# Pairs 4 to 7 of an MLP: transposes on TensorE replaced by a strided reload and 32x32 block transposes on VectorE

## The chip, the core and the metric

The kernel runs on one core of one Trainium2 chip. The metric is the device time of one execution in microseconds (us); the number that counts is the median of several runs. Every figure of an engine, a wait or a transfer comes from one profiled execution.

## The reference, cut to what matters

A transformer block over 2048 tokens of 640 features: a LayerNorm, an attention with a learned feature map, and a second LayerNorm with an MLP (640 to 1728 to 640, squared ReLU). Scale and shift of both norms (`ca`, `sa`, `cb`, `sb`) and both gates come from a small modulation vector.

```python
x = x + ga * attention(layernorm(x) * (1 + ca) + sa)     # x1
h = layernorm(x) * (1 + cb) + sb                         # per token, over 640 features
r = relu(h @ w1 + b1)
x = x + gb * ((r * r) @ w2 + b2)
```

The LayerNorm needs tokens on the partitions (its sums run along the features), while the matrix product with `w1` needs features on the partitions. Between the two, each tile of tokens has to be turned round. The change is about how that is done.

## The kernel before, in words

The attention fills the first 380 us. The MLP then works on pairs of token tiles: pair `j` is 256 tokens, there are eight pairs (0 to 7). All of it is written out in one order by hand (the engines' queues are in program order), in the last loop of the kernel: for pair `j` it goes through seven steps `n`, each with two blocks of 128 hidden features, so fourteen half-steps 0 to 13. In half-step `f`, TensorE computes `up(j, f)` (line 78 by way of `mm`): 15 matmuls of 128x256, three for each of five 128-feature chunks, since each operand is split into a high and a low part. ScalarE applies bias and ReLU (`ft<-up`, L1255), VectorE squares (L1256), ScalarE and VectorE split the result into high (`ra` L1279, `rs` L1295) and low (L88), and TensorE multiplies by `w2` one step later (`acc`). From pair 2 on the second product uses seven block products per step (`down_pair`), whose weights come in from HBM through four ring buffers that GpSimd fetches (`t_fetch`, L1365).

Beside this, while pair `j` is multiplied, pair `j+1` is prepared. `layer(j+1, at)` is called once in each half-step `at`, and the tables `LN_AT0` to `LN_AT` say what is due in which one. For pairs 4 to 7 the table is `LN_AT`, and the work is:

- half-step 0: `load_xm` and `load_xx` load the attention's result (`xm`) and the raw input (`xx`), token tiles of 128x640, by the SP queue.
- half-steps 3 and 4: `add_x` adds the two tiles on VectorE (L1079); the sum is x1, which SP also stores to HBM (`X1`, L1080) for the residual that is needed an iteration later (`residual`, `xr<-x`, L1414).
- half-steps 4 to 7: `ln_pieces` on ScalarE: two sums (L1503), two sums of squares (L1508), and after three small GpSimd operations (L1510 to L1512) two scalings in place (L1515). The sums' unneeded outputs go into `xx`.
- half-steps 8, 10 and 12: `t2`: TensorE transposes two, two and one 128-feature chunks (`t_in`, L357, two transposes for each chunk, into the PSUM tile `tb`); `t_out` applies the modulation on ScalarE (L368, out of PSUM into `xx`), copies to the high part `h` (L369), and VectorE makes the low part (L88 `h<-xx`).

The next pair's `up` reads `h` from half-step 0 on. A chunk `d` is the features 128d to 128d+127, and `w1`'s rows and the modulation's columns `cols_b` are laid out by the same chunks (`mod_turn` transposes the summed modulation rows, parts 3 and 4 being those of `cols_b`).

`row("s1", ...)` hands out five rotating buffers of 128x640; before the change an iteration takes four of them (two `xx`, two `xr`).

Of the kernel before, what the change touches and what calls it, by code (L numbers as in the profile page):

```python
# [22 lines left out]
NC = D // P  # L23
# [9 lines left out]
EPS = 1e-5  # L33
# [2 lines left out]
KEPT = NT - POSTPONED  # L36
W2_AT = 48
PLAIN = 2
DIRECT = 2
LAST = 3  # L40
W_AT = (
# [10 lines left out]
def kernel(  # L52
# [19 lines left out]
    nc = tc.nc  # L72
# [14 lines left out]
    def lo(out_lo, full, hi, eng=None):  # L87
        (eng or nc.vector).tensor_tensor(out_lo, full, hi.bitcast(F32), op=ALU.subtract)  # L88
# [10 lines left out]
    tiny = ctx.enter_context(tc.tile_pool(name="tiny", bufs=1))  # L99
# [17 lines left out]
    def row(tag, name):  # L117
        return (pc if tag in ("s3", "s4") else mem).tile([P, D], F32, tag=tag, name=name, bufs=BUFS[tag])
# [13 lines left out]
    def small(shape, tag, name, bufs=2):  # L132
        return (pc if tag in ("mx", "sk", "dn", "dd") else tiny).tile(shape, F32, tag=tag, name=name, bufs=bufs)
# [4 lines left out]
    def tp(name):  # L138
        return psA.tile([P, 512], F32, tag="tp", name=name)
# [20 lines left out]
    ident = const.tile([P, P], F32, name="ident")  # L160
# [5 lines left out]
    mhalf = const.tile([P, 2], F32, name="mhalf")  # L166
# [4 lines left out]
    cols_b = const.tile([P, 10], F32, name="cols_b")  # L171
# [128 lines left out]
    def mod_turn(part, p, *cs_):  # L300
        t = MT.setdefault(part, None) or row("s1", f"mt{part}")
        MT[part] = t
        a, n = cs_[0] * P, len(cs_) * P
        for i, c in enumerate(cs_):
            nc.tensor.transpose(p[:, i * P : (i + 1) * P], MA[part][:, c * P : (c + 1) * P], ident)
        nc.scalar.activation(t[:, a : a + n], p[:, :n], AF.Copy)

    def mod_sum(part, dest):
# [8 lines left out]
    MA = {}  # L317
# [34 lines left out]
        for _ in ln_parts(xt, nm, spare):  # L352
            pass

    def t_in(xn, d, p):
        for i in range(2):
            nc.tensor.transpose(p[:, i * P : (i + 1) * P], xn[:, i, d * P : (d + 1) * P], ident)  # L357

    def t_unit(xn, cols, hT, d, nm, p=None):
        if p is None:  # L360
            p = tp(f"t{nm}_{d}")
        t_in(xn, d, p)
# [13 lines left out]
    X1 = [dram.tile([P, 2, D], F32, name=f"x1_{j}") for j in range(NT // 2)]  # L376
# [336 lines left out]
    for t in range(2, NT - 2):  # L713
        j, i = divmod(t, 2)
# [12 lines left out]
        p = proj("v", t, (1, 0, lambda: t1(j + 1, 4)) if t == NT - 3 else None)  # L727
# [76 lines left out]
    def bank(nm):  # L804
        return psB.tile([P, 512], F32, tag="m", name=nm)
# [145 lines left out]
    def num_lo(j):  # L951

        if j >= DIRECT:
            for b, (src, hi, low) in enumerate(num_parts(j)):
# [77 lines left out]
    todo = {"load": list(preps), "hi": list(preps), "lo": list(preps)}  # L1032
# [21 lines left out]
    XM, H2, R2 = {}, {}, {}  # L1054

    XX = {}
# [25 lines left out]
    def t2(j, *ds):  # L1082
        if 0 in ds:
            H2[j] = ht(f"h2_{j}", j, (0, 96))
        if j == 0:
            t_unit(XM[j], cols_b, H2[j], ds[0], f"b{j}", bank(f"tb{j}_{ds[0]}"))
            return
        p = tp(f"tb{j}_{ds[0]}")
        for k, d in enumerate(ds):
            t_in(XM[j], d, p[:, 256 * k : 256 * k + 256])  # L1090
# [42 lines left out]
    for j in range(NB):  # L1133
        nxt = j + 1 < NB
        b, c = 2 * j + 5, 2 * j + 6
# [51 lines left out]
        if j == 7:  # L1187
            t2(0, 4)
            p = tp("gbt")[:NC, :P]
# [73 lines left out]
    def plain(j, n):  # L1263
        return j < PLAIN or n == NF // 2 - 1 or j == NB - 1 and n >= NF // 2 - LAST

# [224 lines left out]
    LN2 = {}  # L1490
# [1 line left out]
    LN_AT0 = {"load": 2, "xx": 3, "add": (5, 6), "ln": (5, 6, 7, 7, 8, 9), 10: (0, 1), 11: (2, 3), 12: (4,)}  # L1492
    LN_AT1 = {"load": 3, "add": (5, 5), "ln": (5, 6, 6, 7, 8, 8), 9: (0, 1), 11: (2, 3), 12: (4,)}
    LN_AT2 = {"load": 0, "xx": 3, "add": (6, 6), "ln": (7, 7, 8, 8, 9, 9), 10: (0, 1), 11: (2, 3), 12: (4,)}
    LN_AT = {"load": 0, "add": (3, 4), "ln": (4, 5, 6, 6, 7, 7), 8: (0, 1), 10: (2, 3), 12: (4,)}
    PREPS = iter([1, 3] + [2, 1, 2, 2, 1, 2] + [1, 1] + [1, 2])

    def ln_pieces(xt, nm, spare):
        sm = small([P, 2], "sm", f"sm{nm}")
        sq = small([P, 2], "sq", f"sq{nm}")  # L1500
        nb = small([P, 2], "nb", f"nb{nm}")
        for i in range(2):
            nc.scalar.activation(spare[i], xt[:, i], AF.Identity, accum_out=sm[:, i : i + 1])  # L1503
            if i:
                nc.gpsimd.tensor_scalar(sm, sm, -1.0 / D, None, op0=ALU.mult)
            yield
        for i in range(2):
            nc.scalar.activation(spare[i], xt[:, i], AF.Square, bias=sm[:, i : i + 1], accum_out=sq[:, i : i + 1])  # L1508
            if i:
                nc.gpsimd.tensor_scalar(sq, sq, 1.0 / D, EPS, op0=ALU.mult, op1=ALU.add)  # L1510
                nc.gpsimd.tensor_tensor(sq, sq, mhalf, op=ALU.pow)
                nc.gpsimd.tensor_tensor(nb, sm, sq, op=ALU.mult)  # L1512
            yield
        for i in range(2):
            nc.scalar.activation(xt[:, i], xt[:, i], AF.Identity, bias=nb[:, i : i + 1], scale=sq[:, i : i + 1])  # L1515
            yield

    def layer(j, at, part=None):
        todo = {1: LN_AT0, PLAIN: LN_AT1, PLAIN + 1: LN_AT2}.get(j, LN_AT)
        if j == NB:  # L1520
            return
        if part != 1:
            if at in todo:
                t2(j, *todo[at])
            if todo["load"] == at:
                load_xm(j)
            if todo.get("xx", todo["load"]) == at:
                load_xx(j)
            for i in range(2):
                if todo["add"][i] == at:  # L1530
                    add_x(j, i)
        if part == 0:
            return
        for i in range(6):
            if todo["ln"][i] == at:
                if i == 0:
                    LN2[j] = ln_pieces(XM[j], f"b{j}", XX[j])
                next(LN2[j])

    for j in range(NB):  # L1540
        if j <= PLAIN:
# [4 lines left out]
        for n in range(NP):  # L1546
# [13 lines left out]
            if j < PLAIN:  # L1560
                layer(j + 1, 2 * n, None if j else 0)
# [141 lines left out]
```

## Time and profile before

| what | value |
|---|---|
| median of 3 runs | 766.31 us (765.49 to 766.42) |
| time of the profiled execution | 766.05 us |
| its span in the profile | 764.3 us (1.7 us lie around it) |
| TensorE matmul busy | 758.5 us, 99% of the span |
| VectorE / ScalarE / GpSimd busy | 78% / 57% / 19% |
| granted TensorE clock | 1.00 in each of the four stages looked at (522.8 to 706.7 us) |

Times in the timelines below are microseconds from the span's start. A timeline line gives the start, the length and the instruction, and in square brackets how long its engine had been idle and what ended that. A line of the groups gives, after the bar, the busy time of the whole group in us, the mean length of one instruction in ns, and the idle time before the group. The half-steps of pair 3, in which pair 4 is prepared, lie at 527.8 to 573.6 us; pairs 4, 5 and 6 follow at about 46 us each, and pair 7, in which nothing more is prepared, ends the program.

### The profile page before, as it was taken

What the parts mean: (1) busy time and instruction counts of PE and PEld (TensorE: products, weight loads), DVE (VectorE), ACT (ScalarE), POOL (GpSimd) and SP (SyncE); (2) the same over time, 40 slices, a digit from 0 to 9 for tenths busy, and PEclk for the clock granted to TensorE, in tenths of its full rate; (3) what the DMA queues carried; (4) which work ended last, traced back from release to release, by engine and by line L of the source; (5) the groups of instructions that cost most, each with busy time, mean ns of one, the idle gap of its engine ahead of it and who ended that gap; (6) DMA issues with size and microseconds to landing.
All of it is one profiled execution on the core that took longest, in us unless ns stands there. A gap on an engine that the chain in (4) does not pass through costs nothing.

```text
span 764.3 us, 15303 instructions
## 1 busy us (share of the span) xinstructions
PE 758.5 (99%) x5968; PEld 739.7 (97%) x5968; DVE 593.9 (78%) x1083; ACT 435.6 (57%) x972; POOL 144.9 (19%) x301
## 2 busy tenths in 40 slices
PE   9999999999999999999999999999999999999997
PEld 8999999999999989988999999999999999999997
DVE  6598897988999899999655667876767666685666
ACT  5766756677853364546776647465563645536331
POOL 3001101001100255432101000231321313213110
PEclk9999999999999999999999999999999999999999
DMA  8811431343332345223366466996766759767460
GB/s 322 329 61 78 138 104 54 104 136 112 126 104 93 109 150 188 72 87 104 122 194 221 120 227 236 283 334 209 224 166 207 232 179 268 199 184 204 126 184 35
DMA packets 51505, 126.69 MB, mean 166 GB/s; under 512 B 6684, under 2 KB 7457, under 8 KB 51433
## 3 DMA queue, kind: packets, MB, share of 16 engines
q1 hardware_dynamic: 34098, 84.65, 32.8%
q0 software_dynamic: 14752, 35.76, 16.9%
q10 hardware_dynamic: 2583, 5.30, 1.8%
q8 instruction: 47, 0.77, 0.5%
q14 instruction: 25, 0.20, 0.1%
HBM read 95.70 MB, written 29.89 MB: 164 GB/s over the span
## 4 chain that ended last, share of the span: by engine, by line
PE 91%; DVE 7%; DMA 1%; issue 0%; SPq 0%; ACT 0%; DVEq 0%
PE up L78 24%; PE acc L78 18%; PE pq L78 9%; PE pk L78 9%; PE pv L78 9%; PE pwo L78 6%; PE acc3x L78 5%; PE kvp L450 3%; PE te L920 1%; DVE dn L878 1%; DVE scr L876 1%; DVE ezb L900 1%; PE tb L357 1%; PE ta L357 1%; DVE ot L88 1%; PE foldq L280 1%
## 5 line engine op out<-in xcount | busy, mean ns | idle before, releaser
L78 PE MATMUL up<-h,w 128*128 128x256 f32 x1640 | 206.4, 278 | 0.0
L78 PEld LDWEIGHTS up<-h,w 128*128 128x128 f32 x1640 | 196.1, 188 | 0.0
L1255 ACT ACTIVATE ft<-up,b_t 128x256 f32<-128x256 f32 x104 | 49.1, 472 | 113.8 <-PE up L78 113.2
L78 PE MATMUL acc<-w,ra 128*128 128x384 f32 x452 | 97.4, 335 | 0.0
L1256 DVE TENSOR_TENSOR ft<-ft 128x256 f32<-128x256 f32 x104 | 44.1, 424 | 48.4 <-ACT ft L1255 46.8
L78 PE MATMUL pwo<-wo,ot 128*128 128x256 f32 (+3 forms) x512 | 80.5, 312 | 0.1
L78 PEld LDWEIGHTS pwo<-wo,ot 128*128 128x128 f32 (+1 forms) x512 | 74.4, 188 | 3.2 <-issue 2.7
L78 PE MATMUL pq<-wq,hT 128*128 128x384 f32 (+1 forms) x480 | 75.2, 312 | 0.0
L78 PEld LDWEIGHTS acc<-w,ra 128*128 128x128 f32 x452 | 72.7, 188 | 0.8 <-DVE ra L88 0.5
L78 PE MATMUL pk<-wk,hT 128*128 128x384 f32 (+1 forms) x480 | 72.7, 308 | 0.0
L78 PE MATMUL pv<-wv,hT 128*128 128x384 f32 (+1 forms) x480 | 71.7, 307 | 0.0
L78 PEld LDWEIGHTS pq<-wq,hT 128*128 128x128 f32 x480 | 71.1, 188 | 0.6 <-issue 0.2
L78 PEld LDWEIGHTS pk<-wk,hT 128*128 128x128 f32 x480 | 70.5, 188 | 0.4 <-issue 0.2
L78 PEld LDWEIGHTS pv<-wv,hT 128*128 128x128 f32 x480 | 70.1, 188 | 0.0
L88 DVE TENSOR_TENSOR ra<-ft,ra 128x384 fp32r<-128x384 f32 (+2 forms) x86 | 36.8, 449 | 32.6 <-ACT ra L1279 19.3
L1365 POOL DMA_DIRECT2D ring_a<-td_a x34 | 18.3, 539 | 126.1 <-PE acc L78 100.4
L1279 ACT ACTIVATE ra<-ft 128x384 fp32r<-128x384 f32 x48 | 25.2, 526 | 28.4 <-DVE ft L1256 22.4
L78 PE MATMUL acc3x<-w,ra 128*128 128x256 f32 x231 | 39.8, 278 | 0.0
L78 PEld LDWEIGHTS acc3x<-w,ra 128*128 128x128 f32 x231 | 37.2, 188 | 0.2 <-DVE ra L88 0.2
L1270 DVE TENSOR_TENSOR ft<-ft 128x128 f32<-128x128 f32 x136 | 33.4, 287 | 1.2
L441 DVE TENSOR_REDUCE sk<-ek 128x64 f32<-128x1280 f32 x16 | 23.7, 1484 | 12.4 <-ACT ek L436 10.8
L884 POOL TENSOR_TENSOR dn<-dn,rs_q 128x32 f32<-128x32 f32 x32 | 20.2, 630 | 66.7 <-DVE dn L878 66.4
(270 smaller groups left out, 1412.6 us busy)
## 6 DMA issues: line engine op xcount, KB each, us to landing
ring_c<-td_c POOLq DMA_DIRECT2D x34, 384.0 KB, 4.2
ring_a<-td_a POOLq DMA_DIRECT2D x34, 384.0 KB, 4.1
ring_b<-td_b POOLq DMA_DIRECT2D x34, 256.0 KB, 4.0
esp<-eq SPq DMA_DIRECT2D x12, 640.0 KB, 3.0
el<-esp SPq DMA_DIRECT2D x12, 640.0 KB, 3.9
rw<-in_w SPq DMA_DIRECT2D x23, 320.0 KB, 2.9
wm<-in_w_mod SPq DMA_DIRECT2D x20, 320.0 KB, 3.3
xb<-in_x SPq DMA_DIRECT2D x8, 640.0 KB, 4.2
```

The lines of the kernel that those rows point to most:

```text
L78: nc.tensor.matmul(o, a, b, start=first and i == 0, stop=last and i == len(terms) - 1, skip_group_check=skip,)
L88: (eng or nc.vector).tensor_tensor(out_lo, full, hi.bitcast(F32), op=ALU.subtract)
L280: nc.tensor.matmul(p[g // 3][:, (g % 3) * 120 : (g % 3) * 120 + n], r, bd_t[:120, g * 120 : g * 120 + n], start=True, stop=True,)
L357: nc.tensor.transpose(p[:, i * P : (i + 1) * P], xn[:, i, d * P : (d + 1) * P], ident)
L441: nc.vector.tensor_reduce(s, heads(flat(e)), axis=AX.X, op=ALU.add)
L450: nc.tensor.matmul(kvp[g // 4][64 * c : 64 * c + 64, a : a + 2 * n].rearrange("p (s n) -> p s n", s=2), v[:, u], e[:, :, o : o + n], start ...
L884: nc.gpsimd.tensor_tensor(dn[:, s], dn[:, s], rs[:, 1 - s], op=ALU.mult)
L1255: nc.scalar.activation(r, p, AF.Relu, bias=b1_t[:, f : f + 1])
L1256: nc.vector.tensor_tensor(r, r, r, op=ALU.mult)
L1270: nc.vector.tensor_tensor(t[:, o], t[:, a], t[:, b], op=op)
L1279: nc.scalar.activation(a[:, 0, :3], t[:, :3], AF.Copy)
L1365: nc.gpsimd.dma_start(RING[j, n, r], TD[n][r].bitcast(F32R))
```

## The change

For pairs 4 to 7 (`DEALT = 4`) no transpose is left on TensorE. Instead:

- `add_x`'s second tile moves from half-step 4 to 3, and the sums and squares move to half-steps 4, 4, 5 and 5. Their unneeded outputs go to a fifth row of `s1` (`junk`).
- half-step 5: `load_dealt` reads x1 back from HBM into `xx`, eight DMAs of 32 partitions: partition 32q+t gets, for each of four groups `a` of 32 tokens, the 160 features 160q to 160q+159 of token 32a+t.
- half-step 6: the two LayerNorm factors of each token are copied between partitions, 16 VectorE copies of 32x4, so that partition 32q+t holds those of the tokens 32a+t.
- half-steps 7 and 8: eight scalings of 128x160 on ScalarE, in place in `xx`.
- half-steps 8 and 9: `turn`: one VectorE transpose in 32x32 blocks for each token tile, from `xx` (read with a step of 5 elements, 20 bytes) into `xm`. The feature that ends on partition p of chunk b is 5p+b.
- half-steps 10, 11 and 12: `t_out` for two, two and one chunks, now out of SBUF, in place in `xm`.

Chunks are therefore the features 5p+b, for all pairs. `w1` is laid out so on the host. Pairs 0 to 3 still transpose on TensorE, now reading every fifth element (`by_turn`), 40 transposes; so do the ten of `mod_turn` for parts 3 and 4.

```diff
+DEALT = 4
...
+            src = by_turn(MA[part])[:, c] if part in (3, 4) else MA[part][:, c * P : (c + 1) * P]
+            nc.tensor.transpose(p[:, i * P : (i + 1) * P], src, ident)
...
+    def by_turn(ap):
+        return ap.rearrange("p (f b) -> p b f", b=NC)
...
+    def t_in(xn, d, p, mixed=False):
         for i in range(2):
-            nc.tensor.transpose(p[:, i * P : (i + 1) * P], xn[:, i, d * P : (d + 1) * P], ident)
+            src = by_turn(xn[:, i])[:, d] if mixed else xn[:, i, d * P : (d + 1) * P]
+            nc.tensor.transpose(p[:, i * P : (i + 1) * P], src, ident)
...
+        if j >= DEALT:
+            for d in ds:
+                hf = XM[j].rearrange("p s d -> p (s d)")[:, 256 * d : 256 * d + 256]
+                t_out(cols_b, H2[j], d, f"b{j}", hf, hf)
+            return
...
+    def load_dealt(j):
+        for i in range(2):
+            for q in range(4):
+                nc.sync.dma_start(
+                    XX[j][i][32 * q : 32 * q + 32].rearrange("t (a c) -> t a c", a=4),
+                    X1[j][:, i, 160 * q : 160 * q + 160].rearrange("(a t) c -> t a c", a=4),
+                )
+
+    def turn(j, i):
+        xt = XM[j].rearrange("p s d -> p (s d)").rearrange("p (b i a t) -> p i a b t", b=NC, i=2, t=32)
+        nc.vector.transpose(xt[:, i], XX[j][i].rearrange("p (a t b) -> p a b t", a=4, t=32))
...
-    LN_AT = {"load": 0, "add": (3, 4), "ln": (4, 5, 6, 6, 7, 7), 8: (0, 1), 10: (2, 3), 12: (4,)}
+    LN_AT = {"load": 0, "add": (3, 3), "dealt": 5, "ln": (4, 4, 5, 5, 6, 7, 8), "turn": (8, 9), 10: (0, 1), 11: (2, 3), 12: (4,)}
...
+    def ln_dealt(j):
...
+        for a in range(4):
+            for q in range(4):
+                nc.vector.tensor_copy(ra[32 * q : 32 * q + 32, a], rn[32 * a : 32 * a + 32])
+        yield
+        for i in range(2):
+            for a in range(4):
+                x = XX[j][i][:, 160 * a : 160 * a + 160]
+                nc.scalar.activation(x, x, AF.Identity, bias=ra[:, a, i, 1:2], scale=ra[:, a, i, 0:1])
+            yield
...
-    w1 = np.stack([np.tile(w, (1, P // w.shape[1])).reshape(NC, P, P).transpose(1, 0, 2) for w in w1])
+    w1 = np.stack([np.tile(w, (1, P // w.shape[1])).reshape(P, NC, P) for w in w1])
```

On TensorE the rows below are half-steps 8 and 9 of pair 3, first before and then after the change; `tb` is the PSUM tile of the transposes, `xm` the normalised x1 of pair 4.

```order
L78 MATMUL up<-h_3_6494,w_8_4803 128x256 x15
L78 MATMUL acc_3_6739<-w_6_4898,ra_3_6942 128x384 x3
L78 MATMUL acc_3_6743<-w_7_4943,ra_3_6942 128x384 x3
L78 MATMUL acc_3_6747<-ring_3_c,ra_3_6942 128x384 x3
L357 MATMUL tb_0_7000<-ident,xm_6665 128x128 x4
L78 MATMUL up<-h_3_6494,w_9_4861 128x256 x15
```

```order
L79 MATMUL up<-h_3_6494,w_8_4803 128x256 x15
L79 MATMUL acc_3_6739<-w_6_4898,ra_3_6967 128x384 x3
L79 MATMUL acc_3_6743<-w_7_4943,ra_3_6967 128x384 x3
L79 MATMUL acc_3_6747<-ring_3_c,ra_3_6967 128x384 x3
L79 MATMUL up<-h_3_6494,w_9_4861 128x256 x15
```

The four transposes are gone, and so are the four of half-step 10 and the two of half-step 12; nothing else moves on TensorE.

On VectorE, half-steps 5 to 10 of pair 4, in which pair 5 is prepared; `rn` and `rna` are the factors before and after the copies, `xr` the residual. Before:

```order
L1256 TENSOR_TENSOR ft_3_7472<-ft_3_7472 128x2x128
L88 TENSOR_TENSOR rs_2_7475<-ft_2_7389,rs_2_7475 128x512
L1256 TENSOR_TENSOR ft_3_7472<-ft_3_7472 128x256
...
L88 TENSOR_TENSOR rs_3_7558<-ft_3_7472,rs_3_7558 128x512
L88 TENSOR_TENSOR h_5_7572<-xx_0_7241,h_5_7572 128x256
L88 TENSOR_TENSOR h_5_7572<-xx_1_7242,h_5_7572 128x256
L1256 TENSOR_TENSOR ft_4_7555<-ft_4_7555 128x256
L88 TENSOR_TENSOR ra_4_7601<-ft_4_7555,ra_4_7601 128x384
L1270 TENSOR_TENSOR ft_4_7555<-ft_4_7555 128x128 x4
L1256 TENSOR_TENSOR ft_5_7639<-ft_5_7639 128x2x128
```

And after:

```order
L1279 TENSOR_TENSOR ft_3_7506<-ft_3_7506 128x2x128
L89 TENSOR_TENSOR rs_2_7509<-ft_2_7411,rs_2_7509 128x512
L1561 COPY rna_7430<-rn_7429 32x4 x16
L1279 TENSOR_TENSOR ft_3_7506<-ft_3_7506 128x256
...
L89 TENSOR_TENSOR rs_3_7605<-ft_3_7506,rs_3_7605 128x512
L1115 STREAM_TRANSPOSE xm_7258<-xx_0_7261 128x4x5x32
L1279 TENSOR_TENSOR ft_4_7602<-ft_4_7602 128x256
L89 TENSOR_TENSOR ra_4_7641<-ft_4_7602,ra_4_7641 128x384
L1293 TENSOR_TENSOR ft_4_7602<-ft_4_7602 128x128 x4
L1115 STREAM_TRANSPOSE xm_7258<-xx_1_7262 128x4x5x32
L1279 TENSOR_TENSOR ft_5_7680<-ft_5_7680 128x2x128
```

Sixteen copies come in behind the low part `rs` of half-step 6, one block transpose takes the place of the two `h` of half-step 8, and the other stands behind the sums (L1293) of half-step 9. The `h` of the pair now come in half-steps 10, 11 and 12.

On the SP queue, the same iteration after the change; `x_5` is x1 of pair 5 in HBM, `y` an output row of pair 3.

```order
L1086 DMA x_5_225<-xm_7258 128x640 x2
L1444 DMA out<-y_1_7266 128x640
L1108 DMA xx_0_7261<-x_5_225 32x4x160 x4
L1108 DMA xx_1_7262<-x_5_225 32x4x160 x4
L1437 DMA xr_4_0_7539<-x_4_224 128x640
L1437 DMA xr_4_1_7541<-x_4_224 128x640
```

The eight `xx` DMAs are new and stand between a store of `y` and the two residual loads; the rest of SP's order is as it was.

More of the change, by code (lines that the diff above doesn't have):

```diff
@@ L304, in mod_turn @@
         for i, c in enumerate(cs_):
-            nc.tensor.transpose(p[:, i * P : (i + 1) * P], MA[part][:, c * P : (c + 1) * P], ident)
+            src = by_turn(MA[part])[:, c] if part in (3, 4) else MA[part][:, c * P : (c + 1) * P]
+            nc.tensor.transpose(p[:, i * P : (i + 1) * P], src, ident)
         nc.scalar.activation(t[:, a : a + n], p[:, :n], AF.Copy)
@@ L353, in layer_norm @@
             pass
-    def t_in(xn, d, p):
+    def by_turn(ap):
+        return ap.rearrange("p (f b) -> p b f", b=NC)
+    def t_in(xn, d, p, mixed=False):
         for i in range(2):
-            nc.tensor.transpose(p[:, i * P : (i + 1) * P], xn[:, i, d * P : (d + 1) * P], ident)
+            src = by_turn(xn[:, i])[:, d] if mixed else xn[:, i, d * P : (d + 1) * P]
+            nc.tensor.transpose(p[:, i * P : (i + 1) * P], src, ident)
     def t_unit(xn, cols, hT, d, nm, p=None):
@@ L361, in t_unit @@
             p = tp(f"t{nm}_{d}")
-        t_in(xn, d, p)
+        t_in(xn, d, p, True)
         t_out(cols, hT, d, nm, p)
@@ L1087, in t2 @@
             return
+        if j >= DEALT:
[3 more added lines that the diff above has]
+            return
         p = tp(f"tb{j}_{ds[0]}")
         for k, d in enumerate(ds):
-            t_in(XM[j], d, p[:, 256 * k : 256 * k + 256])
+            t_in(XM[j], d, p[:, 256 * k : 256 * k + 256], True)
         for k, d in enumerate(ds):
             t_out(cols_b, H2[j], d, f"b{j}", p[:, 256 * k : 256 * k + 256], XX[j][d % 2][:, :256])
+    def load_dealt(j):
[8 more added lines that the diff above has]
+        nc.vector.transpose(xt[:, i], XX[j][i].rearrange("p (a t b) -> p a b t", a=4, t=32))
     NB = NT // 2
@@ L1516, in ln_pieces @@
             yield
+    def ln_dealt(j):
+        sm = small([P, 2], "sm", f"smb{j}")
+        rn = tiny.tile([P, 2, 2], F32, tag="rn", name=f"rn{j}", bufs=1)
+        ra = tiny.tile([P, 4, 2, 2], F32, tag="rna", name=f"rna{j}", bufs=1)
+        sq, nb = rn[:, :, 0], rn[:, :, 1]
+        junk = row("s1", f"junk{j}")
+        for i in range(2):
+            nc.scalar.activation(junk, XM[j][:, i], AF.Identity, accum_out=sm[:, i : i + 1])
+            if i:
+                nc.gpsimd.tensor_scalar(sm, sm, -1.0 / D, None, op0=ALU.mult)
+            yield
+        for i in range(2):
+            nc.scalar.activation(junk, XM[j][:, i], AF.Square, bias=sm[:, i : i + 1], accum_out=rn[:, i, 0:1])
+            if i:
+                nc.gpsimd.tensor_scalar(sq, sq, 1.0 / D, EPS, op0=ALU.mult, op1=ALU.add)
+                nc.gpsimd.tensor_tensor(sq, sq, mhalf, op=ALU.pow)
+                nc.gpsimd.tensor_tensor(nb, sm, sq, op=ALU.mult)
+            yield
+        for a in range(4):
+            for q in range(4):
+                nc.vector.tensor_copy(ra[32 * q : 32 * q + 32, a], rn[32 * a : 32 * a + 32])
+        yield
+        for i in range(2):
+            for a in range(4):
+                x = XX[j][i][:, 160 * a : 160 * a + 160]
+                nc.scalar.activation(x, x, AF.Identity, bias=ra[:, a, i, 1:2], scale=ra[:, a, i, 0:1])
+            yield
     def layer(j, at, part=None):
@@ L1533, in layer @@
             return
-        for i in range(6):
-            if todo["ln"][i] == at:
+        for i in range(2):
+            if j >= DEALT and todo["turn"][i] == at:
+                turn(j, i)
+        for i, k in enumerate(todo["ln"]):
+            if k == at:
                 if i == 0:
-                    LN2[j] = ln_pieces(XM[j], f"b{j}", XX[j])
+                    LN2[j] = ln_dealt(j) if j >= DEALT else ln_pieces(XM[j], f"b{j}", XX[j])
                 next(LN2[j])
+        if todo.get("dealt") == at:
+            load_dealt(j)
     for j in range(NB):
```

## The prediction

> **What bounds the kernel now.** I read the page's busy shares first, then the chain of work that ended last, then TensorE's timeline around the transposes that go.
>
> ```profile
> PE 758.5 (99%) x5968; PEld 739.7 (97%) x5968; DVE 593.9 (78%) x1083; ACT 435.6 (57%) x972; POOL 144.9 (19%) x301
> PE 91%; DVE 7%; DMA 1%; issue 0%; SPq 0%; ACT 0%; DVEq 0%
> ```
>
> TensorE has work in 99% of the span, and 91% of the chain is its own instructions. "Busy" alone would not prove a bound, since the ends of matmuls are modelled; the chain does, and so do the starts below, which follow each other without a gap. In the MLP, then, an instruction taken off TensorE is worth its own time, as long as VectorE, ScalarE and the transfers still deliver ahead of it. The next lines are TensorE's timeline in the iteration of pair 3, in which pair 4 is prepared, with lines of unchanged matmuls left out.
>
> ```profile
> 550.18 1.87 PE L78 MATMUL up<-h,w 128*128 128x256 f32 x15
> 551.88 0.68 PE L78 MATMUL acc<-ring_a,rs 128*128 128x384 f32 x3
> ...
> 553.42 1.86 PE L78 MATMUL up<-h,w 128*128 128x256 f32 x15
> ...
> 556.68 0.60 PE L357 MATMUL tb<-ident,xm 128*128 128x128 f32 x4
> 557.04 2.01 PE L78 MATMUL up<-h,w 128*128 128x256 f32 x15
> 558.89 0.69 PE L78 MATMUL acc<-ring_a,rs 128*128 128x384 f32 x3
> ...
> 560.45 1.86 PE L78 MATMUL up<-h,w 128*128 128x256 f32 x15
> ...
> 563.72 0.60 PE L357 MATMUL tb<-ident,xm 128*128 128x128 f32 x4
> 564.07 1.96 PE L78 MATMUL up<-h,w 128*128 128x256 f32 x15
> ...
> 567.41 1.86 PE L78 MATMUL up<-h,w 128*128 128x256 f32 x15
> ...
> 570.67 0.38 PE L357 MATMUL tb<-ident,xm 128*128 128x128 f32 x2
> 570.80 1.43 PE L78 MATMUL up<-h,w 128*128 128x256 f32 x10
> ...
> 572.07 0.69 PE L78 MATMUL acc<-ring_a,rs 128*128 128x384 f32 x3
> ...
> 573.63 1.86 PE L78 MATMUL up<-h,w 128*128 128x256 f32 x15
> ```
>
> Read starts, not lengths, since neighbouring matmuls overlap. An undisturbed odd half-step lasts 553.42 - 550.18 = 3.24, and its 15 matmuls of `up` 1.70, that is 0.113 each.
>
> **What goes: 5.1.** The first four transposes put 557.04 - 556.68 = 0.36 between their neighbours, and the half-step behind them lasts 560.45 - 557.04 = 3.41, which is 0.17 too long. Together 0.53. The second four: 0.35, and 567.41 - 564.07 = 3.34, 0.10 too long; 0.45. The last two: 0.13, and 573.63 - 570.80 = 2.83 against 3.24 - 5 x 0.113 = 2.67 for a half-step with ten `up`; 0.29. That is 1.27 for a pair, and four pairs lose these ten transposes: **5.1 us** off TensorE.
>
> **What stays there and changes its form: 0.3.** Fifty transposes (40 of pairs 0 to 3, ten of the modulation) now load their weights with a step of 20 bytes. No row of the trace shows a strided load. These are the nearest:
>
> ```profile
> L78 PEld LDWEIGHTS up<-h,w 128*128 128x128 f32 x1640 | 196.1, 188 | 0.0
> L450 PEld LDWEIGHTS kvp<-ek,vt 128*64 128x64 f32 x352 | 19.0, 137 | 1.0
> L586 PEld LDWEIGHTS mrow<-wm,cs 128*32 128x32 f32 x100 | 3.0, 109 | 0.5 <-PE kvp L357 0.2 <-PE pk L78 0.2
> L357 PEld LDWEIGHTS tb<-ident,xm 128*128 128x128 f32 x80 | 9.8, 140 | 0.6
> ```
>
> An ordinary load costs 109, 137 and 188 ns for 32, 64 and 128 columns: about 0.82 ns a column on top of 83. A transpose's load of 128 columns costs only 140, so 57 of streaming. If a step of 20 bytes doubles that to 114, the load looks like those of `up`, which hide behind a matmul every 113 ns; transposes come every 0.5/4 = 0.13 us, so next to nothing is seen. If it is four times (228), each transpose lasts some 0.12 longer, 50 x 0.12 = 6 us. If nothing changes, 0. I take the near end, 50 x 6 ns = 0.3.
>
> **What is added on VectorE, and what lies behind it.** The lines are VectorE's in half-steps 6 to 11, then group rows for prices.
>
> ```profile
> 549.91 0.69 DVE L88 TENSOR_TENSOR rs<-ft,rs 128x512 fp32r<-128x512 f32 x1
> 552.59 0.43 DVE L1256 TENSOR_TENSOR ft<-ft 128x256 f32<-128x256 f32 x1 [1.99 <-ACT ft L1255]
> 553.61 0.56 DVE L88 TENSOR_TENSOR ra<-ft,ra 128x384 fp32r<-128x384 f32 x1 [0.59 <-PE acc L78]
> ...
> 556.35 0.69 DVE L88 TENSOR_TENSOR rs<-ft,rs 128x512 fp32r<-128x512 f32 x1
> ...
> 561.13 1.02 DVE L1270 TENSOR_TENSOR ft<-ft 128x128 f32<-128x128 f32 x4
> 562.86 0.43 DVE L1256 TENSOR_TENSOR ft<-ft 128x256 f32<-128x256 f32 x1 [0.71 <-ACT ft L1255]
> ...
> 567.69 0.56 DVE L88 TENSOR_TENSOR ra<-ft,ra 128x384 fp32r<-128x384 f32 x1 [0.59 <-ACT ra L1279]
> ```
>
> ```profile
> L1079 DVE TENSOR_TENSOR xm<-xm,xx 128x640 f32<-128x640 f32 x16 | 12.8, 819 | 0.0
> L294 DVE TENSOR_SCALAR wm<-wm,cs 128x640 f32<-128x640 f32 x4 | 2.2, 548 | 0.0
> L893 DVE TENSOR_TENSOR dn<-rs_q,dd 128x32 f32<-128x32 f32 x32 | 4.7, 189 | 0.5
> ```
>
> The 16 copies stand between `rs` (ends 550.60) and the square at 552.59, in 1.99 us of idle time. The nearest row, `dn`, is 189 ns long and 147 apart (4.7/32), so 2.4 to 3.0 us in all, less if four elements cost less than 32. They end up to 1.0 late; the `ra` that follows ended at 554.17 and TensorE begins on it some 0.95 later (half-step 7's `acc`, 1.70 behind the `up` of 553.42), so this is just covered. I take 0.
>
> A block transpose reads 640 elements. Its bounds are 0.55 (`wm`) and four times 0.82 (`xm`, if each 20-byte step cost four accesses); I take 0.82, the row of one element at a time. The first stands behind `rs` (ends 557.04), where the two `h` of half-step 8 stood, and TensorE's earlier start there still leaves it 1.5. The second stands in the 0.71 before 562.86 and so holds the square by about 0.1.
>
> From there slack is thinner than before. TensorE is 0.98 earlier by half-step 11, while VectorE still has the residual's bias and two `h` ahead of that half-step's square, and ScalarE now has two chunks' `t_out` (four instructions) in half-step 11, where it had none. `ra` of half-step 11 ended at 568.25 and was used at 569.11 (1.70 behind the `up` of 567.41); it now has about 0.5 of these 0.86 left. `rs` of half-step 12, used at 572.07, is left about 0.3. I take 0.1 a pair, **0.4**, with 0 and 2.0 (0.5 a pair) as ends.
>
> **What is added on SP and ScalarE, and the wait in it.** SP's and ScalarE's timelines:
>
> ```profile
> 549.40 0.34 SPq L1421 DMA_DIRECT2D out<-y  x1
> 549.79 1.06 SPq L1414 DMA_DIRECT2D xr<-x  x2
> ```
>
> ```profile
> 553.05 0.53 ACT L1279 ACTIVATE ra<-ft 128x384 fp32r<-128x384 f32 x1 [0.49 <-DVE ft L1256]
> 553.48 1.72 ACT L1515 ACTIVATE xm<-xm,nbb,sqb 128x640 f32<-128x640 f32 x2
> 555.32 0.48 ACT L1255 ACTIVATE ft<-up,b_t 128x256 f32<-128x256 f32 x1
> 555.70 0.62 ACT L1295 ACTIVATE rs<-ft 128x512 fp32r<-128x512 f32 x1
> ```
>
> ```profile
> ring_a<-td_a POOLq DMA_DIRECT2D x34, 384.0 KB, 4.1
> ...
> a<-at ACTq DMA_DIRECT2D x16, 320.0 KB, 2.2
> ...
> xr<-x SPq DMA_DIRECT2D x16, 320.0 KB, 5.1
> ```
>
> SP is in order, so the eight loads wait for the store of `y` at 549.40. At 0.53 each (1.06 for two), the fourth is issued from about 551.4. To landing takes between 2.2 (`a`) and 5.1 (`xr`): 553.6 to 556.5. ScalarE wants to start scaling at 553.6, when four of 128x160 replace two of 128x640 (1.72); the square's `ft` and `rs` are queued behind it. That `rs` goes through VectorE's low part (ends 557.04) to TensorE's `acc` of 558.89, now 558.36, so the loads may land until about 554.9 before TensorE notices. Each moves only 80 KB, which is nearer to `a` than to 320 KB of `xr` on a busy queue; with 3.0 they land at 554.4. I take 0; the far end, 1.6 a pair, is 6.4 us. The residual loads, 4 us later, are wanted only in half-step 10.
>
> The added 640 KB a pair also pass beside the ring that GpSimd fetches in the same half-step:
>
> ```profile
> 550.75 0.58 POOL L1365 DMA_DIRECT2D ring_a<-td_a  x1 [2.39 <-PE acc L78]
> ```
>
> It is the one used at 558.89, now 558.36; at the median of 4.1 it lands at 554.9 and has 3.5 in hand. I price it at nothing; were its 4.1 doubled, TensorE would lose 0.6 a pair, 2.4 us.
>
> **The sum.** Profiled time 766.05 - 5.1 + 0.3 + 0.4 = 761.65. The median is 0.26 above that execution, so **761.9**. With the small ends it is 761.2; with half a microsecond a pair lost in half-steps 11 and 12, 763.5.
>
> **The rivals.**
> 1. *ScalarE waits for the reloaded rows.* The mechanism is the one above: decided at a landing at 554.9, in half-step 7. Between there and 556.5 it costs 0 to 6.4 us: 762 to 768.3, in the middle 765. For it: SP's loads are strided and many. Against: they are small.
> 2. *Strided reads at half rate.* Weight loads stay hidden; a block transpose takes 1.5, and of the 0.7 more, about 0.4 a pair comes through behind the second one: 763.5.
> 3. *Strided reads at a quarter of the rate, the slower side.* The place is the second block transpose. From about 1.5 us long it makes the square of half-step 10, the `h` behind it and so `ra` of half-step 11 late; each further microsecond is one microsecond a pair. At 3.3 us that is some 1.8 a pair, 7 us, and with 6 us on the fifty weight loads 775; on VectorE alone, 769. For it: no strided read in the trace shows the opposite. Against: contiguous reads of four bytes show no limit near.
>
> On 2 and 3 the Trainium skill has a rule that speaks against the change: SBUF — State Buffer, Door 1: The DMA port swizzle, says that SBUF is read in lines of 16 bytes, that full rate needs at least two hits on a line, and that four-byte elements may therefore lie at most four apart. Five apart, every access is a new line; by that rule the time is that of rival 2 or 3. The page has no price, and the trace of before holds no such read, so it neither agrees nor disagrees.
>
> **How the numbers follow.** A measurement of this kernel can tell about 0.2%, 1.5 us, from no change: faster is below 764.8, slower above 767.8. Chances: the forecast 0.45 (761.0 to 763.5), a little better than it 0.05, rival 1 0.22 (0.07 of it faster, 0.11 within, 0.04 slower), rival 2 0.12 (0.09 faster, 0.03 within), rival 3 0.16 (slower). Faster 0.66, same 0.14, slower 0.20. For 8 in 10 the range runs from 760.6 to 769.0, which leaves out most of rival 3.
>
> **What would show it.** Right: TensorE's starts follow on at 0.113 through half-steps 8 to 13, and a pair takes 1.27 less. Rival 1: idle time of ScalarE before the scalings, released by a DMA on `xx`, and TensorE waiting for `rs` in half-step 9. Rivals 2 and 3: STREAM_TRANSPOSE at 1.5 or 3.3 us, the loads of `tb` of pairs 1 to 3 above 200 ns, TensorE waiting for `ra` or `rs` in half-steps 11 and 12. The forecast is wrong, too, if TensorE is seen to wait for a ring.

## The result: slower, 779.35 us, and the profile after

The changed kernel takes 779.35 us (median of 4 runs, 777.41 to 779.82) against 766.32 before (765.49 to 766.42): a ratio of 1.0166, 95% interval 1.0149 to 1.0182. Forecast were 761.9 and a range up to 769.0, so it is 13 us slower where 4 us faster were expected. The profiled execution took 779.53, its span is 777.8.

First the page's engine line, its chain of work (two lines), and the groups in which `up` and ScalarE's scaling stand (busy time and mean ns, then the idle time before and what ended it):

```profile
PE 763.9 (98%) x5928; PEld 744.9 (96%) x5928; DVE 613.2 (79%) x1155; ACT 442.7 (57%) x996; POOL 145.1 (19%) x301
PE 86%; DVE 7%; DMA 3%; issue 2%; ACT 1%; SPq 1%; POOL 0%; POOLq 0%; ACTq 0%; DVEq 0%
L79 PE MATMUL up<-h,w 128*128 128x256 f32 x1640 | 208.8, 279 | 8.4 <-ACT ft L1278 8.4
```

```profile
L1566 ACT ACTIVATE xx<-xx,rna 128x160 f32<-128x160 f32 x32 | 14.0, 508 | 10.3 <-DMA xx<-x 10.3
```

TensorE has 40 instructions fewer and is busy 5.4 us longer, and now it waits: 8.4 us before `up`, for the ReLU (`ft`, now L1278). ScalarE in turn sat idle for 10.3 us before the scalings, for the reloaded rows. The place where it happens is seen in the timelines, first TensorE's and then ScalarE's, around half-steps 7 and 8 of pair 3. Half-steps of TensorE are numbered here as in the prediction, which is one less than the index `f`: the `up` of 553.42 before and of 556.97 after stands ahead of the first transposes in the order lists, so it is `up(3, 8)`, and the one that waits is `up(3, 9)`.

```profile
556.97 1.89 PE L79 MATMUL up<-h,w 128*128 128x256 f32 x15
558.70 1.22 PE L79 MATMUL acc<-w,ra 128*128 128x384 f32 x6
559.75 0.69 PE L79 MATMUL acc<-ring_c,ra 128*128 128x384 f32 x3
562.37 2.93 PE L79 MATMUL up<-h,w 128*128 128x256 f32 x15 [1.93 <-ACT ft L1278]
565.10 1.16 PE L79 MATMUL acc<-ring_a,rs 128*128 128x384 f32 x3
```

```profile
555.59 0.47 ACT L1278 ACTIVATE ft<-up,b_t 128x256 f32<-128x256 f32 x1 [2.31 <-PE up L79]
557.47 0.53 ACT L1302 ACTIVATE ra<-ft 128x384 fp32r<-128x384 f32 x1 [1.41 <-DVE ft L1279]
560.21 1.75 ACT L1566 ACTIVATE xx<-xx,rna 128x160 f32<-128x160 f32 x4 [2.21 <-DMA xx<-x]
561.87 0.45 ACT L1278 ACTIVATE ft<-up,b_t 128x256 f32<-128x256 f32 x1
```

ScalarE is ready at 557.47 + 0.53 = 558.00 and may scale only at 560.21. The ReLU of half-step 7 is queued behind the scalings and ends at 562.32; only then does TensorE start the next `up` (562.37), since both halves of `up`'s PSUM are one tile and its first matmul waits for the ReLU of the half-step before. That `up` was due 0.52 after the `acc` of 559.75, at 560.27: 2.10 us lost. The same gap stands in the other three pairs: 1.94, 2.58 and 2.39, together **9.0 us**. All four go when the loads come earlier (third experiment).

Two further losses need the granted clock and the pace. A table by stage (length, busy time of five engines, granted clock, DMA share, GB/s):

```profile
559.00:562.40 3.40, 1.47 (x10) 1.15 (x8) 0.54 (x3) 2.19 (x6) 0.53 (x1) 1.00 1.19 293
562.40:567.00 4.60, 4.60 (x24) 4.60 (x25) 2.90 (x5) 3.08 (x7) 0.33 (x1) 0.63 0.58 199
567.00:580.00 13.00, 13.00 (x102) 13.00 (x101) 10.72 (x26) 8.43 (x19) 3.31 (x7) 1.00 0.57 141
```

Behind the first wait, and in this execution behind that one alone, TensorE ran 4.6 us at a mean granted clock of 0.63: 4.6 x (1 - 0.63) = **1.7 us**. The `up` of 562.37 takes 2.73 to the next start in place of 1.70.

And the MLP's matmuls are a little slower, also far from any wait: the `up` of 556.97 takes 558.70 - 556.97 = 1.73, before it was 1.70, and six `acc` take 1.05 in place of 1.04. Aligned by their order, the two executions are already 2.6 us apart at 513 us, before anything was reloaded; 0.4 of it was there when the MLP began.

### The profile page after: what moved, and what is told of

It is laid out like the page before. It is cut to its first block, busy times and chain, and to the rows that moved or that the text cites. A ratio compares the mean times of both kernels' runs of the same rounds, so it can differ in the third digit from the quotient of the medians.

```text
span 777.8 us, 15394 instructions
## 1 busy us (share of the span) xinstructions
PE 763.9 (98%) x5928; PEld 744.9 (96%) x5928; DVE 613.2 (79%) x1155; ACT 442.7 (57%) x996; POOL 145.1 (19%) x301
## 4 chain that ended last, share of the span: by engine, by line
PE 86%; DVE 7%; DMA 3%; issue 2%; ACT 1%; SPq 1%; POOL 0%; POOLq 0%; ACTq 0%; DVEq 0%
PE up L79 22%; PE acc L79 15%; PE pq L79 9%; PE pk L79 9%; PE pv L79 9%; PE pwo L79 5%; PE acc3x L79 5%; PE kvp L456 3%; DMA xx<-x 2%; PE te L926 1%; DVE dn L884 1%; DVE scr L882 1%; DVE ezb L906 1%; PE foldk L281 1%; DMA ring_b<-td_b 1%
## 5 line engine op out<-in xcount | busy, mean ns | idle before, releaser
L79 PE MATMUL up<-h,w 128*128 128x256 f32 x1640 | 208.8, 279 | 8.4 <-ACT ft L1278 8.4
L79 PEld LDWEIGHTS up<-h,w 128*128 128x128 f32 x1640 | 199.0, 189 | 9.9 <-ACT ft L1278 9.6
L1278 ACT ACTIVATE ft<-up,b_t 128x256 f32<-128x256 f32 x104 | 48.8, 469 | 112.6 <-PE up L79 112.4
L79 PEld LDWEIGHTS acc<-w,ra 128*128 128x128 f32 x452 | 74.8, 188 | 0.4 <-DVE ra L89 0.3
L1293 DVE TENSOR_TENSOR ft<-ft 128x128 f32<-128x128 f32 x136 | 33.3, 286 | 1.2
L447 DVE TENSOR_REDUCE sk<-ek 128x64 f32<-128x1280 f32 x16 | 23.7, 1484 | 12.4 <-ACT ek L442 10.8
```

The costliest lines, as they stand in the source:

```text
L79: nc.tensor.matmul(o, a, b, start=first and i == 0, stop=last and i == len(terms) - 1, skip_group_check=skip,)
L447: nc.vector.tensor_reduce(s, heads(flat(e)), axis=AX.X, op=ALU.add)
L1278: nc.scalar.activation(r, p, AF.Relu, bias=b1_t[:, f : f + 1])
L1293: nc.vector.tensor_tensor(t[:, o], t[:, a], t[:, b], op=op)
```

## The experiments

**Theory.** Two things that the diff does not show as a cost make the 13 us. (A) The two new small tiles, `rn` and `rna`, take 96 bytes in a pool that lies below the MLP's own pool; so `ft`, `ra`, `rs`, the late weights and the ring all start 96 bytes higher, and TensorE is slower on them there. (C) The eight loads come too late because SP issues them behind the store of `y`. Rivals: the slower pace comes from what the change adds (B); the transfers are slow however early they start (D). A third, that earlier loads hold up a ring load (E), is seen once, further down.

### The four corners: loads earlier, buffers back in place

The kernel before with the 96 bytes alone; nothing reads or writes them:

```diff
+    tiny.tile([P, 24], F32, name="fill3")
```

> The kernel before, with 96 bytes of unused SBUF added per partition ahead of the pool that holds ft, ra, rs and the ring in the MLP; no instruction changes. Theory A (the change's two small tiles cost time only because they push these buffers 96 bytes up, and TensorE streams them 1 to 2 per cent slower there): 771 to 773 us, 15 `up` take 1.72 to 1.73 us from start to start in place of 1.70, and the last three `acc` of a down part .53 in place of .52. Rival B (the slower pace comes from what the change adds: strided reads, the copies, the reloads, or the clock): 766.3 within 0.5, 15 `up` at 1.70.

Measured: 772.41 us against 766.39, ratio 1.0075 (1.0063 to 1.0087): 6.0 us. TensorE's `up` and its `acc` in the padded kernel, then in the kernel before:

```profile
L78 PE MATMUL up<-h,w 128*128 128x256 f32 x1640 | 208.3, 279 | 0.0
L78 PE MATMUL acc<-w,ra 128*128 128x384 f32 x452 | 98.8, 339 | 0.0
```

```profile
L78 PE MATMUL up<-h,w 128*128 128x256 f32 x1640 | 206.4, 278 | 0.0
L78 PE MATMUL acc<-w,ra 128*128 128x384 f32 x452 | 97.4, 335 | 0.0
```

No instruction differs and none waits (the last column is 0.0), yet both groups are busy longer, by 0.9% and 1.4%. Theory A holds, B falls for these 6 us.

The kernel after, with an existing filler 96 bytes shorter, so that the MLP's buffers lie where they lay before:

```diff
-    tiny.tile([P, 144], F32, name="fill2")
+    tiny.tile([P, 120], F32, name="fill2")
```

> The kernel after, with a filler tile 96 bytes shorter, so that ft, ra, rs and the ring lie where they lay before the change; no instruction changes. Theory A (addresses): 5 to 6.5 us faster than after, 773 to 774.5, 15 `up` back at 1.70, the four waits of TensorE for ft (2.1, 1.9, 2.6, 2.4 us) still there. Rival B (pace follows from the change's instructions): 779 within 1.

Measured: 773.31 (770.49 to 778.20, a ratio to before of 1.0065 to 1.0122), 6.0 below after and uncertain by some 2 us, with the waits in place (1.93, 2.15, 3.98, 2.29 in the profiled execution, which took 778.20). Behind two of them the clock fell: after the third 0.52 from 656.6 to 662.0, 2.6 us lost, and after the fourth 0.86 on the mean of 12 us, 1.7 us. That two such stretches fell into this execution goes with its place at the upper end of a spread of 8 us.

The kernel after, with the loads one half-step earlier, which changes nothing but their place in SP's queue, ahead of the store of `y`:

```diff
-    "dealt": 5
+    "dealt": 4
```

> The kernel after, with the eight loads of a pair issued one even half-step earlier, which puts them ahead of the store of y in SP's queue. Theory C (the loads are late because SP issues them behind that store, at 553.25): all eight land before ScalarE is ready to scale, TensorE's four waits for ft go (9.0 us) and with them the stretch at half clock behind the first (2.0): 768 to 771. Rival D (the loads are late because the transfer engines are shared with the ring, however early they are issued): waits of 1 us and more per pair stay, 774 to 779. Rival E (earlier they collide with a ring load that is wanted sooner): TensorE waits for a ring, 775 to 783.

Measured: 768.52, ratio to before 1.0027 (1.0016 to 1.0039), 10.8 below after. C holds, and D falls as the reason for the wait. ScalarE's scalings in this kernel:

```profile
L1566 ACT ACTIVATE xx<-xx,rna 128x160 f32<-128x160 f32 x32 | 14.0, 508 | 0.0
```

The 10.3 us of idle time before them are gone, and so are TensorE's waits for `ft`.

Both edits at once:

> Both: loads issued one even half-step earlier, and the filler 96 bytes shorter. If A and C hold and add up: 779.35 - 11 - 5.5 = 762 to 764.5, faster than the kernel before by 2 to 4 us. If only C holds: 768 to 771. If only A holds: 773 to 774.5.

Measured: **762.64** (761.34 to 763.03), ratio to before 0.9948 (0.9936 to 0.9959). This version beats both kernels, by 3.75 and 16.7 us. The two causes add up: alone, the edits take 6.0 (A) and 10.8 (C) off the kernel after, 16.8 in sum, and together 16.7. With the loads early, A is worth 768.52 - 762.64 = 5.9. SP's timeline in the four corners' last version:

```profile
546.43 3.90 SPq L1108 DMA_DIRECT2D xx<-x  x8
550.43 0.41 SPq L1444 DMA_DIRECT2D out<-y  x1
550.94 1.40 SPq L1437 DMA_DIRECT2D xr<-x  x2
```

and in the kernel after:

```profile
552.79 0.34 SPq L1444 DMA_DIRECT2D out<-y  x1
553.25 4.10 SPq L1108 DMA_DIRECT2D xx<-x  x8
```

On their own axes the loads start some 4 us earlier against TensorE's half-step 7 (554.13 and 556.97): 7.7 us ahead of it in place of 3.7.

### What about an address costs

The same filler in the kernel before, in other sizes: 64, 32, 512 and 128 bytes.

> The kernel before with 64 unused bytes ahead of the pool of ft, ra, rs and the ring, where the run with 96 took 772.4 against 766.4. The pool then starts 128 bytes above a multiple of 512, in place of 64 before and 160 with 96. Theory F (a start off a multiple of 64 bytes costs time): 128 is such a multiple, so 766.4 within 0.7. Rival G (every move from the place it was tuned to costs, by the distance or by which buffers then fall on one another): 769 to 773.

> The same with 32 unused bytes: the pool starts 96 bytes above a multiple of 512, a multiple of 32 and not of 64. Theory F: about the 6.0 us of the 96 bytes again, 771 to 773, since both starts are 32 past a multiple of 64. Rival G by distance: a third of it, 767.5 to 769.

> The kernel before with 512 unused bytes ahead of the pool of ft, ra, rs and the ring; 32, 64 and 96 gave 774.6, 773.7 and 772.4 in place of 766.4. Theory K (what counts is where a buffer starts modulo 512 or a part of it): 766.4 within 0.7. Rival L (every distance between this pool and the buffers below it that was not tuned costs): 769 to 775.

> The kernel before with 128 unused bytes ahead of the pool of ft, ra, rs and the ring: 32, 64 and 96 cost 6.0 to 8.3 us, 512 nothing. If what counts is the start modulo 128: 766.5 within 0.7. If it is modulo 256 or 512: 769 to 775.

| bytes added | pool's start modulo 512 | time, us | ratio to before, 95% |
|---|---|---|---|
| 0 | 64 | 766.4 | |
| 32 | 96 | 774.63 | 1.0108 (1.0094 to 1.0121) |
| 64 | 128 | 773.67 | 1.0095 (1.0081 to 1.0109) |
| 96 | 160 | 772.41 | 1.0075 (1.0063 to 1.0087) |
| 128 | 192 | 771.44 | 1.0065 (1.0045 to 1.0084) |
| 512 | 64 | 766.44 | 1.0000 (0.9990 to 1.0009) |

Theory F (a multiple of 64 bytes is enough) fell with the first of them. Rival G failed in the form "by distance": 32 bytes cost the most. 512 bytes cost nothing (theory K; rival L falls), 128 cost 5.1 us. So the start counts modulo 512 or 256; which of the two was not tried. Not all of the difference is pace: in the profiled executions with 64 and 32 bytes TensorE also waits 2.1 and 1.8 us for one ring load, near 517 us, and not in the kernel before. So the order among the four starts is not to be read closely.

Then only `ft`, which ScalarE and VectorE read and write but TensorE never does, was moved by 96 bytes modulo 512:

```diff
     p3.tile([P, 2, 4, P], F32, tag="rs", name="rs")
+    p3.tile([P, 24], F32, name="gap4")
...
             FT[j, f // 2] = p3.tile([P, 8, P], F32, tag="ft", name=f"ft{j}_{f // 2}", bufs=2)
+            if (j, f) == (0, 0):
+                p3.tile([P, 104], F32, name="gap5")
```

> The kernel before, in whose pool only the two buffers of ft (written and read by ScalarE and VectorE, never by TensorE) start 96 bytes further modulo 512; ra, rs, the ring and the late weights, which TensorE reads, keep their start modulo 512. Theory M (what costs is where TensorE's own operands start): 766.5 within 0.7. Rival N (what costs is that ScalarE's and VectorE's accesses meet TensorE's in the same places): 768 to 772, part or all of the 6.0 us of the 96 bytes.

Measured: 766.68, ratio 1.0004 (0.9994 to 1.0013). Its group of `up`:

```profile
L78 PE MATMUL up<-h,w 128*128 128x256 f32 x1640 | 206.4, 278 | 0.0
```

206.4 again: theory M, and rival N falls. What costs is the place of the buffers that TensorE reads (or of one of them; they were not moved apart).

### The parts of the change by themselves

Only the new order of the features, so 90 strided transposes on TensorE and nothing on VectorE (`DEALT = 8`, the table `LN_AT` of before):

> Of the change only the new order of the features: all eighty transposes of the MLP and ten of the modulation load their weights with a step of 20 bytes; nothing is reloaded or turned on VectorE, and the buffers lie where they lay before. By the prediction's sum (6 ns each, hidden): 90 x 6 ns = 0.5, 766.9 within 0.5. By the 199 ns that such a load took in the kernel after, 59 more than before, if all of it showed: 90 x 59 ns = 5.3, 771.7. If the next load is hidden by the matmul all the same: 766.4.

Measured: 767.15, ratio 1.0009 (1.0000 to 1.0018), so 0.8 us, with 0 and 1.4 as ends: at most some 9 ns each by the medians. The loads of these transposes:

```profile
L363 PEld LDWEIGHTS tb<-ident,xm 128*128 128x128 f32 x80 | 12.1, 200 | 0.0
```

200 ns in place of 140, as good as hidden.

The kernel after with whole rows in place of the pieces; the features are then not dealt out over the partitions, so what is turned is not the reference's x:

```diff
-            for q in range(4):
-                nc.sync.dma_start(
...
+            nc.sync.dma_start(XX[j][i], X1[j][:, i])
```

> The kernel after, with the eight loads of a pair replaced by two of whole rows (320 KB each in place of four of 80 KB); the rows are then not regrouped, so the turned x is not the reference's. Addresses as after, and behind the store of y as after. Theory H (many small pieces make the loads land late): the two land 3 to 3.5 us after issue, by about 557, and TensorE's waits for ft all but go: 769 to 771. Rival I (the bytes, beside the ring's 384 KB in the same stretch, make them late): the rows land 5 to 6 us after issue, at 558.5 to 559.5 where 560.1 stood, and 0.5 to 1.5 us of each wait of 2.1 to 2.6 stay: 772 to 777.

Measured: 770.10, ratio 1.0043 (1.0029 to 1.0056). The loads in the list of transfers (KB each, median us to landing), first here, then in the kernel after:

```profile
xx<-x SPq DMA_DIRECT2D x8, 320.0 KB, 5.7
```

```profile
xx<-x SPq DMA_DIRECT2D x32, 80.0 KB, 4.9
```

A whole row of 320 KB takes no less than a piece of 80 KB, so theory H fell on its landing: rival I's 5 to 6 us and its 0.5 to 1.5 of wait are what TensorE shows (0.89, 0.89, 0.52 and none). But the time is below I's 772, since in the last two pairs little or nothing of the wait is left and no stretch at a lower clock follows. (Landings are on record for 4 of these 8 loads and for 12 of the 32 pieces.) By this, what the pieces cost is their number on SP: the first tile needs four issues, the last of them 1.5 us after the first.

The faster version without loads and block transposes, so that pairs 4 to 7 are neither regrouped nor turned:

```diff
-    "dealt": 4,
-    "turn": (8, 9),
+    "turn": (99, 99),
```

> The faster version without the eight loads and without the two block transposes: pairs 4 to 7 read their x neither scaled nor turned, so the output is not the reference's. What is left of the change is the 40 transposes removed, the strided weight loads, the copies and the scalings. By the prediction's first term (5.1 us, 1.27 a pair): 766.35 - 5.1 + 0.3 = 761.5. By the steps seen in the faster version's alignment (about 1.1 a pair): 766.35 - 4.4 + 0.3 = 762.2, and then loads and block transposes together cost less than 0.5 there. If they cost more than that: below 761.

Measured: 761.99, ratio 0.9940 (0.9923 to 0.9956). Aligned by their order, TensorE gains 1.25, 1.26, 1.24 and 1.24 us on the kernel before in the four pairs. The faster version gains 1.25, 1.24, 0.57 and 1.24: loads and block transposes cost 0.7 in one pair and nothing in the others, and the medians differ by 0.7, too. It is this wait:

```profile
646.84 1.88 PE L79 MATMUL up<-h,w 128*128 128x256 f32 x15
649.16 0.76 PE L79 MATMUL acc<-ring_a,rs 128*128 128x384 f32 x3 [0.44 <-DMA ring_a<-td_a]
...
650.80 0.39 PE L79 MATMUL up<-h,w 128*128 128x256 f32 x2
```

The half-step takes 650.80 - 646.84 = 3.96 in place of 3.25. That ring load was issued at 641.15, while the eight loads were on their way, and took 7.9 us to land. Those of the other three pairs took 6.1 to 7.2 and landed in time; in the kernel before, the four took 5.3 to 5.7. This is rival E, at 0.7 us in all.

The faster version with the second block transpose twice:

```diff
-        nc.vector.transpose(xt[:, i], XX[j][i].rearrange("p (a t b) -> p a b t", a=4, t=32))
+        for _ in range(1 + i):
+            nc.vector.transpose(xt[:, i], XX[j][i].rearrange("p (a t b) -> p a b t", a=4, t=32))
```

> The faster version (loads ahead of the store of y, filler shortened; 762.6) with the second block transpose of each pair issued twice, so that it takes 2.8 us in place of 1.39. By the prediction's third rival (beyond 1.5 us each further microsecond delays the square, the h behind it and ra of half-step 11 by as much): 1.3 us a pair, 762.6 + 5.2 = 767.8. By this version's own timeline, where rs of half-step 11 ends 1.1 us before TensorE uses it: 0.3 to 1.0 a pair, 764 to 766.6. If VectorE's idle time takes it: 762.6.

Measured: 765.90, ratio to before 0.9993 (0.9984 to 1.0003), so 3.3 more than the faster version, 0.8 a pair on the mean. VectorE's timeline and TensorE's behind it, pair 5:

```profile
607.47 2.77 DVE L1116 STREAM_TRANSPOSE xm<-xx 128x640 f32<-128x640 f32 x2
610.16 0.38 DVE L1280 TENSOR_TENSOR ft<-ft 128x256 f32<-128x256 f32 x1
610.46 0.68 DVE L89 TENSOR_TENSOR rs<-ft,rs 128x512 fp32r<-128x512 f32 x1
```

```profile
609.13 1.87 PE L79 MATMUL up<-h,w 128*128 128x256 f32 x15
612.69 1.98 PE L79 MATMUL up<-h,w 128*128 128x256 f32 x15
616.49 1.43 PE L79 MATMUL up<-h,w 128*128 128x256 f32 x10 [0.17 <-ACT ft L1279]
619.29 1.86 PE L79 MATMUL up<-h,w 128*128 128x256 f32 x15
```

The three half-steps take 3.56, 3.80 and 2.80; undisturbed they take 3.25, 3.25 and 2.68 (rows in the next section). That is 0.98 lost in this pair; two more lose 1.0 and 1.1, and in the first, where TensorE had just lost 0.9 to a late ring load, the second transpose costs 0.1. Rival 3's place and mechanism are right, its price is a little high: 2.77 us is 1.27 beyond 1.5, so 1.27 a pair were due.

## Why the prediction was wrong, point by point

**What goes: right.** The faster version is free of the two faults, so its timeline can be held against the rows of the prediction:

```profile
554.13 1.86 PE L79 MATMUL up<-h,w 128*128 128x256 f32 x15
557.39 1.89 PE L79 MATMUL up<-h,w 128*128 128x256 f32 x15
560.66 1.86 PE L79 MATMUL up<-h,w 128*128 128x256 f32 x15
563.91 1.87 PE L79 MATMUL up<-h,w 128*128 128x256 f32 x15
567.16 1.86 PE L79 MATMUL up<-h,w 128*128 128x256 f32 x15
570.41 1.30 PE L79 MATMUL up<-h,w 128*128 128x256 f32 x10
573.09 1.18 PE L79 MATMUL up<-h,w 128*128 128x256 f32 x9
```

From half-step 7 to 13 it takes 573.09 - 554.13 = 18.96; before it was 573.63 - 553.42 = 20.21. That is 1.25 a pair, forecast 1.27; the version without loads and block transposes gains it in all four pairs, 5.0.

**Strided weight loads: right.** 90 of them cost 0.8 or less, so 50 about 0.4; taken were 0.3. The load itself takes 199 ns in the kernel after, where doubled streaming gave 83 + 114 = 197.

**VectorE: the block transposes were longer than taken, at no cost to TensorE.** Two groups of the kernel after, then the copies of pair 4 and the square behind them:

```profile
L1115 DVE STREAM_TRANSPOSE xm<-xx 128x640 f32<-128x640 f32 x8 | 11.1, 1388 | 0.0
L1561 DVE COPY rna<-rn 32x4 f32<-32x4 f32 x64 | 10.7, 167 | 1.2
```

```profile
554.10 2.88 DVE L1561 COPY rna<-rn 32x4 f32<-32x4 f32 x16
557.01 0.43 DVE L1279 TENSOR_TENSOR ft<-ft 128x256 f32<-128x256 f32 x1
```

A block transpose takes 1.39 and not 0.82, near rival 2's 1.5. By that rival 0.4 a pair should have come through; the half-steps 10 to 12 above take 3.25, 3.25 and 2.68, against 3.24 and 2.67 undisturbed, so nothing does, and not the 0.1 a pair that was taken either. The Trainium skill (SBUF — State Buffer, Door 1: The DMA port swizzle) has it that strides beyond a line of 16 bytes cost. The weight load agrees in direction, 199 ns in place of 140; no run here has this block transpose without the step. Neither decided anything here.

The sixteen copies took 2.88 in pair 4, inside the forecast 2.4 to 3.0, and held the square until 557.01, 0.95 behind the end of the ReLU (556.06). The prediction counted only TensorE as waiting for that. But ScalarE's `ra` waits for the square, too (the 1.41 in its timeline), and the scalings stand behind `ra`: they were ready 0.9 later. By itself this cost nothing: at 558.00 the rows had not landed, and with early loads the copies are still there and no wait is.

**The loads: here it failed.** The term was 0, with "taken 3.0" from issue to landing, and it is 10.8 us. Half-step 7 begins 556.97 - 553.42 = 3.55 later on the axis of after, which has to be taken off:
- Issue: forecast 549.79 for the first and 551.4 for the fourth; measured 553.25 - 3.55 = 549.70 and 554.73 - 3.55 = 551.18. Right.
- Landing: the fourth landed at 560.10, 5.4 after its issue, which is beyond even the far end of 5.1; on the axis of before that is 556.55, where 554.4 was forecast. 3.0 was chosen because a piece has only 80 KB, nearer to `a`. But the 16 loads of `a` that gave 2.2 were issued from 278 to 389 us, ahead of the ring's first load at 479. The whole rows of 320 KB, with 5.7 against 4.9, show that in this stretch the size hardly matters. In the faster version the loads take as long (median 5.3) and have the time.
- Latest landing without loss: forecast 554.9, found by the `rs` that `acc` uses at 558.36. The first in TensorE to suffer was not this `acc` but the next `up`, which waits for the ReLU behind the scalings. It was due at 560.27, and from the start of the scalings to its own start pass 562.37 - 560.21 = 2.16; so they had to start by 558.11 and the rows to land by 558.00, which is 554.45 on the axis of before.
- Loss: 556.55 - 554.45 = 2.10. The step that failed is the landing, taken 2.15 too early (3.0 where 5.4 was measured). By the forecast's own limit it would have cost 1.65; that the limit is 0.45 earlier makes it 2.10.

So rival 1 is what happened, in the half-step that it named, through another operand. Its price was too small: 1.9 to 2.6 a pair in place of at most 1.6. The 1.7 of lower clock behind a wait was in no term; with the 9.0 of waits it makes 10.7 of the 10.8.

**The ring: nearly right.** Priced at nothing, with 4.1 to landing; in the faster version the four loads beside the reloads take 6.1 to 7.9 us and one of them cost TensorE 0.7.

**What was not there at all: 5.9 us.** The sum starts from the time of before and lets everything else in the MLP stay as it was. The table of addresses shows that this step is wrong: what a change allocates below the buffers that TensorE reads moves them, and four of the five shifts tried here cost 5.1 to 8.3 us.

With the measured sizes: 766.3 - 5.0 + 0.4 + 0.7 (loads and block transposes when in time) = 762.4, and the version free of the two faults took 762.64, inside the forecast's own range of 761.0 to 763.5. With 10.8 and 5.9 on top it is 779.1, against 779.35; this second sum tests little, since both sizes are differences between these very kernels.

## What to carry to other kernels

When an edit puts a transfer on a queue in program order, work out when the engine that waits for it must go on for *each* of its consumers (a ReLU that frees PSUM among them), and take the landing from the busiest transfers of that stretch, not from the smallest; here one place earlier in SP's queue was worth 10.8 us. When a kernel's pace changes far from the edit, compare the addresses of the buffers before any theory on the engines: fill the pool up so that TensorE's operands start at the same place modulo 512. Idle time on an engine does not make an added instruction free: doubling the second block transpose, 1.38 us, cost 0.8 a pair.

## What the runs showed of the hardware that was not expected

- **Starts of TensorE's operands.** With fp32 operands, 32 to 128 bytes of shift cost 5.1 to 8.3 us of some 380 us of MLP (up to 2.1 of it a wait for one ring load), 512 bytes cost nothing, and moving a buffer that TensorE does not read cost nothing. `up`, which reads none of the moved buffers itself, is slower, too (208.3 against 206.4 busy). The Trainium skill (SBUF — State Buffer, Operand start alignment) gives a rule for where operands may start and says that its runs timed nothing; these do. The attention shows no such loss: its pool `pc` moves by the same bytes and TensorE reads fp32 from it, too, but the MLP's first `up` starts at 387.68 with 96 bytes and at 387.70 without. Why it is so was not shown.
- **The clock after a short wait.** A wait of 2.1 us was followed by 4.6 us at a mean of 0.63, the only one of four in the execution of after; with the buffers back in place it was two of four, behind waits of 4.0 and 2.3. What decides it was not shown. The Trainium skill (TensorE: Matmul & The Clock Gate, Why this matters for your kernels) advises against idle gaps over about 3 us; here 2.1 was enough once, and 1.9 to 2.6 in the other places of the same two executions was not.
- **Landing under load.** From SP, 80 KB in pieces and 320 KB in whole rows took about the same (medians 4.9 and 5.7 us) while the ring moved 1 MB a step. In the attention, ahead of the ring, 320 KB of `a` by ScalarE's queue took 2.2.
